# A decode attention kernel on one core: all K ahead of all V in shared buffers, MLP between the V groups, and four denominator matmuls for eight

## Chip, cores, metric

One NeuronCore of a Trainium2 chip. The metric is device time in microseconds of one execution. The profile's span (first to last instruction) is shorter than the time of the same execution in the kernel before (2.6 in its profile). Ratios compare runs of the same chip and call; where microseconds of two kernels are set against each other, the calls may differ, and the ratios to the kernel before say how far that holds. "Fast" means within 1.5% of the fastest of the same kernel, "slow" the rest.

## The reference, cut to what matters

```python
W = 1024                       # of 4096 cached positions, the last 1024
q = (layernorm(x) @ wq)        # B = 4, one new token, 32 query heads, 8 K/V heads, head size 128
scores = q @ k[:, :, -W:].T * 128 ** -0.5
o = softmax(scores) @ v[:, :, -W:]
s = o @ wo                     # 4096 -> 512
h = gelu(layernorm(xn) @ w1 + b1)        # 512 -> 1792
g = silu(h @ w2 + b2)                    # 1792 -> 512
return x + s * g
```

All is bf16. Per K/V head ("group") there is 1 MiB of K and 1 MiB of V over the four batch rows; wq and wo have 4 MiB each, w1 and w2 1.75 MiB each: 27.5 MiB (28.8 MB) to be read once, with little arithmetic.

## The kernel before: the parts concerned

Everything is requested from one queue, K and V alternating, four buffers each; a new K or V waits for the matmuls that free its buffer.

```python
NKN = 4; NV = 4; NKT = 6; NP = 3          # buffers: K, V, transposed K, probabilities
load_k(0)
d_wq = [...]                               # four DMAs of 1 MiB
load_v(0); load_k(1); d_w1 = ...; load_v(1); load_k(2); d_w2 = ...; load_v(2); load_k(3); load_v(3)
```

One unit is 256 positions of a group for all four batch rows: eight 128x128 transposes by the tensor engine (PE), one copy out of PSUM by the vector engine (DVE), eight score matmuls.

```python
def T(n): ...   # 8 transposes into psK, then a DVE copy to kt_buf
def S(n): ...   # 8 score matmuls (before the first of a group: a 512-column mask fill); after the 4th unit Exp on ACT
def PV(g):      # 32 matmuls v.T @ P, then the denominator:
    for k in range(8):
        pe.matmul(pso[:, 32:96], ones_bf, P_buf[:, g % NP, k * 64:(k + 1) * 64], ...)
for n in range(4, NUN + LAG + 1):          # LAG = 2
    T(n); S(n - LAG)
    if last unit of a group: PV(g - 1)     # mlp1 after the first, mlp3 after the second
    ...
rows1 = to_rows(0, 6)                      # head outputs, reshuffled for the projection
PV(7); ...
for k in range(3): wo(k, rows1)            # 96 projection matmuls, groups 0 to 5
rows2 = to_rows(6, 8)
for k in range(3, 6): wo(k, rows2)         # 32 more
```

The softmax here doesn't subtract the row's maximum and nothing guards it: scores larger than these inputs give would overflow.

Of the kernel before, what the change touches and what calls it, by code (L numbers as in the profile page):

```python
# [16 lines left out]
class _Program:  # L17
# [10 lines left out]
    def add(self, eng, fn, *deps):  # L28
        op = _Op(eng, fn, deps)
        self.ops[eng].append(op)  # L30
        return op
# [42 lines left out]
def bass_recurrent_scan__sliding_block_cached__mixer_channel_mlp__decode_kernel(  # L74
# [26 lines left out]
    FC = F // 128  # L101
# [1 line left out]
    KR = W // NC  # L103
    UT = 8
    NU = NC // UT
    NKN = 4
    NV = 4
    NKT = 6
    NP = 3
    NB = 3  # L110
    SCALE = DH ** -0.5
    GELU_A = 1.5957691216057308
# [39 lines left out]
    OW = sb([128, 4, HKV * 4], BF16)  # L152
    hT = sb([128, FC * 4], BF16)

    kn_buf = sb([128, NKN, NC, DH], BF16)
    v_buf = sb([128, NV, NC, DH], BF16)
    kt_buf = sb([128, NKT, UT * 128], BF16)
    P_buf = sb([128, NP, NC * 16], BF16)
    OTb = sb([128, HKV * 16], BF16)
    den_sb = sb([128, HKV * 16], F32)  # L160
    rden = sb([128, HKV * 16], F32)
# [31 lines left out]
    def cache_rows(cache, g):  # L193

        return bass.AP(cache.tensor, g * SK * DH + WS * DH,
                       [[NC * DH, KR], [HKV * SK * DH, B], [1, NC * DH]])
# [4 lines left out]

    def load_k(g):
        d_k[g] = pg.dma("sp", "k%d" % g, lambda e: e.dma_start(  # L203
            kn_buf[:, g % NKN, :, :].rearrange("p c d -> p (c d)"), cache_rows(A_k_cache, g)),
            t_last[g - NKN] if g >= NKN else None)

    def load_v(g):
        d_v[g] = pg.dma("sp", "v%d" % g, lambda e: e.dma_start(  # L208
            v_buf[:, g % NV, :, :].rearrange("p c d -> p (c d)"), cache_rows(A_v_cache, g)),
            pv_op[g - NV] if g >= NV else None)  # L210

    load_k(0)
    wq_r = A_wq.rearrange("(p c) n -> p c n", c=4)
    d_wq = [pg.dma("sp", "wq%d" % c, lambda e, c=c: e.dma_start(  # L214
        wq_sb[:, c, :], wq_r[:, c, :])) for c in range(4)]
    load_v(0)
    load_k(1)
    d_w1 = pg.dma("sp", "w1", lambda e: e.dma_start(
        w1_sb[:, :, :], B_w1.rearrange("(p c) f -> p c f", c=4)))
    load_v(1)  # L220
    load_k(2)
    d_w2 = pg.dma("sp", "w2", lambda e: e.dma_start(
        w2_sb[:, :, :], B_w2.rearrange("(p c) o -> p c o", c=FC)))
    load_v(2)
    load_k(3)
    load_v(3)

    x_r = A_x.rearrange("b s (c p) -> (b s c) p", p=128)


# [46 lines left out]
    def T(n):  # L277
        g, u = n // NU, n % NU

        def fn(pe):  # L280
            last = None
            for j in range(UT):
                last = pe.transpose(psK[n % NB][:, j * 128:(j + 1) * 128],  # L283
                                    kn_buf[:, g % NKN, u * UT + j, :], ident[:, :])
            return last
        t = add("pe", fn, d_k[g], c_id, cp.get(n - NB), v_xyT if n >= 4 else None)
        if u == NU - 1:
            t_last[g] = t
        cp[n] = add("dve", lambda e: e.tensor_copy(kt_buf[:, n % NKT, :], psK[n % NB][:, 0:1024]),  # L289
                    t, sc.get(n - NKT))  # L290

    def S(n):
        g, u = n // NU, n % NU

        def fn(pe):
            last = None
            if u == 0:
                pe.matmul(psS[g % 2][:, 0:512], ind[:, :], negm[:, :], start=True, stop=False,  # L298
                          skip_group_check=True)
            for j in range(UT):  # L300
                c = u * UT + j
                last = pe.matmul(psS[g % 2][:, c * 16:(c + 1) * 16],  # L302
                                 kt_buf[:, n % NKT, j * 128:(j + 1) * 128],
                                 qT[:, g * 16:(g + 1) * 16],
                                 start=False, stop=(c == NC - 1), skip_group_check=True)
            return last
        sc[n] = add("pe", fn, cp[n], v_q, c_neg, c_ind,
                    ex[g - 2] if u == 0 and g >= 2 else None)
        if u == NU - 1:
            ex[g] = add("act", lambda e: e.activation(  # L310
                P_buf[:, g % NP, :], psS[g % 2][:, 0:512], AF.Exp, scale=SCALE),
                sc[n], den[g - NP] if g >= NP else None)

    def PV(g):
        pso = psO[g % 2]

        def fn(pe):
            last = None
            for c in range(NC):
                last = pe.matmul(pso[:, 0:16], v_buf[:, g % NV, c, :],  # L320
                                 P_buf[:, g % NP, c * 16:(c + 1) * 16],
                                 start=(c == 0), stop=(c == NC - 1))
            return last
        pv_op[g] = add("pe", fn, ex[g], d_v[g], ep[g - 2] if g >= 2 else None)

        def fd(pe):
            last = None
            for k in range(8):
                last = pe.matmul(pso[:, 32:96], ones_bf[:, :],  # L329
                                 P_buf[:, g % NP, k * 64:(k + 1) * 64],  # L330
                                 start=(k == 0), stop=(k == 7))
            return last
        den[g] = add("pe", fd)

    def epilogue(g):
        pso = psO[g % 2]
        cs = slice(g * 16, (g + 1) * 16)
        v = add("dve", lambda e: e.tensor_reduce(  # L338
            den_sb[:, cs], bass.AP(pso, 32, [[512, 128], [1, 16], [16, 4]]),
            AX.X, ALU.add), den[g])  # L340
        v = add("dve", lambda e: e.reciprocal(rden[:, cs], den_sb[:, cs]), v)  # L341

        ep[g] = add("dve", lambda e: e.tensor_tensor(
            bass.AP(OTb, g * 16, [[HKV * 16, 128], [1, 4], [4, 4]]),
            pso[:, 0:16], rden[:, cs], ALU.mult), v, pv_op[g])


    v_xyT = None
    for n in range(4):
        T(n)  # L350

    def f_xy(pe):
# [3 lines left out]
                last = pe.transpose(psK[1][:, s + c * 4:s + c * 4 + 4],  # L356
                                    bass.AP(src, c, [[512, 4], [4, 128]]), ident[0:4, 0:4])
        return last
    t_xy = add("pe", f_xy, v_xn, v_y, c_id, cp[3])
    v_xyT = add("dve", lambda e: e.tensor_copy(xyT[:, :], psK[1][:, 0:32]), t_xy)  # L360

    def f_q(pe):
# [15 lines left out]
    def mlp1():  # L378
        def fn(pe):
            last = None  # L380
            for k in range(FC):
                o = psM[:, PS_H + k * 4:PS_H + (k + 1) * 4]
                for c in range(4):
                    pe.matmul(o, bass.AP(w1_sb, c * F + k, [[4 * F, 128], [FC, 128]]),  # L384
                              xyT[:, 16 + c * 4:16 + (c + 1) * 4], start=(c == 0), stop=False)
                last = pe.matmul(o, bass.AP(b1_sb, k, [[F, 1], [FC, 128]]), ones_bf[0:1, 0:4],  # L386
                                 start=False, stop=True)
            return last
        h = psM[:, PS_H:PS_H + FC * 4]
        t = add("pe", fn, v_xyT, d_w1, d_b1)  # L390
        a = add("act", lambda e: e.activation(u2_sb[:, :], h, AF.Square), t)  # L391
        v = add("dve", lambda e: e.tensor_scalar(t_sb[:, :], u2_sb[:, :], GELU_K, 1.0,  # L392
                                                 op0=ALU.mult, op1=ALU.add), a)
        v = add("dve", lambda e: e.tensor_tensor(t2_sb[:, :], t_sb[:, :], h, ALU.mult), v)
        mlp["e"] = add("act", lambda e: e.activation(ge_sb[:, :], t2_sb[:, :], AF.Exp,
                                                     scale=-GELU_A), v)

    def mlp2():
        h = psM[:, PS_H:PS_H + FC * 4]
        v = add("dve", lambda e: e.tensor_single_scalar(e1_sb[:, :], ge_sb[:, :], 1.0, ALU.add),  # L400
                mlp["e"])
        v = add("dve", lambda e: e.reciprocal(r_sb[:, :], e1_sb[:, :]), v)
        mlp["h"] = add("dve", lambda e: e.tensor_tensor(hT[:, :], h, r_sb[:, :], ALU.mult), v)
# [20 lines left out]
        mlp["g"] = add("dve", lambda e: e.tensor_tensor(  # L424
            g_sb[:, :], psM[:, PS_Z:PS_Z + 16], rz_sb[:, :], ALU.mult), v)

    LAG = 2
    NUN = HKV * NU
    for n in range(4, NUN + LAG + 1):
        g, u = n // NU, n % NU  # L430
        if n < NUN:
            T(n)
        if n - LAG < NUN:
            if n == 4:
                S(0)
                S(1)
            S(n - LAG)
        if u == NU - 1 and 1 <= g:
            PV(g - 1)
            if n == 7:  # L440
                mlp1()
            if n == 11:
                mlp3()
            if g - 1 + NV < HKV:
                load_k(g - 1 + NKN)
                load_v(g - 1 + NV)
        if u == 0 and g >= 2 and n < NUN:
            epilogue(g - 2)
        if n == 9:
            mlp2()  # L450
        if n == 14:
            mlp4()

    wo_r = A_wo.rearrange("(g p i) o -> p g i o", g=HKV, i=4)
    d_wo = []
# [41 lines left out]
            return last  # L497
        return add("pe", fn, d, rows, mlp["g"])

    rows1 = to_rows(0, 6)  # L500
    epilogue(HKV - 2)
    PV(HKV - 1)
    epilogue(HKV - 1)
    for k in range(3):
        wo(k, rows1)
    rows2 = to_rows(6, 8)
    for k in range(3, len(d_wo)):
        t_w = wo(k, rows2)


    v = add("dve", lambda e: e.tensor_tensor(
# [61 lines left out]
```

## Time and profile before

| | before |
|---|---|
| time, three runs | 80.37, 80.77, 80.80 us |
| span of the profiled execution (82.2 us, a slow one) | 79.6 us |
| bytes, mean rate from 2 to 70.5 us | 28.8 MB, 418 GB/s |
| last byte | about 72.0 us |
| end of the last projection matmul | 76.8 us |
| PE stops without a wait ("issue") of over half a us | 0.81, 1.96, 2.16 us |

In a line of the chain of waits, the first number is the start, the second the duration, then the engine, the tile written, and how many instructions were merged. "issue" is time for which the profile shows no reason. In a line by stage: window, its length, then busy time (and instructions) of PE, PE weight load, DVE, ACT, POOL, then clock, DMA share and GB/s. The lines themselves stand in the prediction below.

### The profile page before, as it was taken

The numbers are of one execution on the slowest core, as the hardware profiler recorded it, in microseconds if no ns is written. First come the engines' busy times: TensorE is split into PE (matmuls) and PEld (weight loads), VectorE is DVE, ScalarE is ACT, GpSimd is POOL, SyncE is SP. The second block draws the span as 40 slices with busy tenths as digits, with TensorE's granted clock in tenths as the row PEclk, the third lists the DMA queues.
The fourth block names the chain that finished last, engine by engine and source line by source line (L and its number), as shares of the span: only waits on it lengthen the run. The fifth ranks groups of instructions, "written<-read, shape, count | busy, mean of one in ns | idle before, by whom it ended". The sixth has DMA issues, their size and how long they took to land.

```text
span 79.6 us, 2723 instructions
## 1 busy us (share of the span) xinstructions
PE 56.5 (71%) x1267; PEld 52.9 (66%) x1267; DVE 32.7 (41%) x82; ACT 8.4 (11%) x15; POOL 4.3 (5%) x12
## 2 busy tenths in 40 slices
PE   0029510097089999999999999969819999708860
PEld 0029310096079999999899899969718999608850
DVE  0788900002033600029811886929636368403010
ACT  0617000000002000023000302003003020300000
POOL 6950000000000000000000000000000000000000
PEclk9999995555555999655697589999995599965555
DMA  0999999999999999999999999999999999971000
GB/s 2 339 425 401 433 424 428 424 424 460 412 425 416 420 429 446 402 416 412 437 420 437 399 437 416 420 404 420 424 408 420 410 414 422 414 286 56 0 0 2
DMA packets 4502, 29.01 MB, mean 365 GB/s; under 512 B 518, under 2 KB 523, under 8 KB 1676
## 3 DMA queue, kind: packets, MB, share of 16 engines
q1 hardware_dynamic: 4448, 28.84, 87.2%
q8 instruction: 9, 0.15, 0.7%
q10 hardware_dynamic: 44, 0.01, 0.1%
q14 instruction: 1, 0.01, 0.0%
HBM read 28.85 MB, written 0.00 MB: 363 GB/s over the span
## 4 chain that ended last, share of the span: by engine, by line
PE 62%; DMA 22%; issue 7%; SPq 4%; DVE 1%; ACT 1%
PE psK L283 23%; DMA kn_buf<-in_A_k_cache_dram 22%; PE psO L320 9%; PE psS L302 8%; PE psM L384 6%; PE psM L491 4%; PE psS L298 3%; PE psO L329 3%; SPq L214 3%; PE psM L386 3%; PE psM L411 2%; SPq L203 1%; ACT P_buf L310 1%; SPq L208 1%; PE psM L413 1%
## 5 line engine op out<-in xcount | busy, mean ns | idle before, releaser
L283 PE MATMUL psK<-ident,kn_buf 128*128 128x128 bf16 x256 | 25.3, 261 | 10.4 <-DMA kn_buf<-in_A_k_cache_dram 8.4
L289 DVE COPY kt_buf<-psK 128x1024 bf16<-128x1024 bf16 x32 | 21.2, 684 | 16.4 <-PE psK L283 16.4
L283 PEld LDWEIGHTS psK<-ident,kn_buf 128*128 128x128 bf16 x256 | 19.6, 118 | 10.8 <-DMA kn_buf<-in_A_k_cache_dram 8.5
L302 PEld LDWEIGHTS psS<-qT,kt_buf 128*128 128x128 bf16 x256 | 11.0, 103 | 1.8 <-issue 1.3
L302 PE MATMUL psS<-qT,kt_buf 128*128 128x16 bf16 x256 | 11.4, 174 | 0.0
L320 PE MATMUL psO<-P_buf,v_buf 128*128 128x16 bf16 x256 | 7.8, 170 | 2.6 <-issue 2.2
L310 ACT ACTIVATE P_buf<-psS 128x512 bf16<-128x512 f32 x8 | 4.8, 598 | 41.0 <-PE psS L302 41.0
L320 PEld LDWEIGHTS psO<-P_buf,v_buf 128*128 128x128 bf16 x256 | 7.1, 96 | 2.8 <-issue 2.2
L366 PE MATMUL psM<-xyT,wq_sb 128*128 128x4 bf16 x128 | 3.6, 166 | 5.4 <-DMA wq_sb<-in_A_wq_dram 5.4
L366 PEld LDWEIGHTS psM<-xyT,wq_sb 128*128 128x128 bf16 x128 | 3.5, 104 | 5.5 <-issue 5.5
L384 PE MATMUL psM<-xyT,w_sb 128*128 128x4 bf16 x56 | 5.6, 204 | 0.0
L384 PEld LDWEIGHTS psM<-xyT,w_sb 128*128 128x128 bf16 x56 | 4.4, 154 | 0.2
L298 PE MATMUL psS<-negm,ind 128*128 128x512 bf16 x8 | 4.0, 506 | 0.1
L329 PE MATMUL psO<-P_buf,ones_bf 128*128 128x64 bf16 x64 | 3.5, 197 | 0.8 <-issue 0.8
L372 DVE CAST qT<-psM 128x128 bf16<-128x128 f32 x1 | 0.4, 435 | 8.8 <-PE psM L366 8.8
L491 PE MATMUL psM<-OW,wo_sb 128*128 128x4 bf16 x128 | 3.7, 166 | 0.4 <-DVE OW L477 0.4
L491 PEld LDWEIGHTS psM<-OW,wo_sb 128*128 128x128 bf16 x128 | 3.6, 105 | 0.5 <-issue 0.5
L392 DVE TENSOR_SCALAR t_sb<-u_sb 128x56 f32<-128x56 f32 x1 | 0.2, 192 | 7.4 <-ACT u_sb L391 7.4
L329 PEld LDWEIGHTS psO<-P_buf,ones_bf 128*128 128x128 bf16 x64 | 2.6, 100 | 0.9 <-issue 0.9
L338 DVE TENSOR_REDUCE den_sb<-psO 128x16 f32<-128x64 f32 x8 | 1.7, 216 | 3.3 <-PE psO L329 3.3
L386 PE MATMUL psM<-ones_bf,b_sb 1*128 1x4 bf16 x14 | 3.0, 215 | 0.0
L341 DVE RECIPROCAL rden<-den_sb 128x16 f32<-128x16 f32 x8 | 2.0, 253 | 0.3
(57 smaller groups left out, 27.0 us busy)
## 6 DMA issues: line engine op xcount, KB each, us to landing
kn_buf<-in_A_k_cache_dram SPq DMA_DIRECT2D x8, 1024.0 KB, 19.7
v_buf<-in_A_v_cache_dram SPq DMA_DIRECT2D x8, 1024.0 KB, 17.1
wq_sb<-in_A_wq_dram SPq DMA_DIRECT2D x4, 1024.0 KB, 9.5
w_sb<-in_B_w_dram SPq DMA_DIRECT2D x2, 1792.0 KB, 24.7
wo_sb<-in_A_wo_dram SPq DMA_DIRECT2D x3, 1024.0 KB, 14.8
wo_sb<-in_A_wo_dram SPq DMA_DIRECT2D x1, 512.0 KB, 17.4
wo_sb<-in_A_wo_dram SPq DMA_DIRECT2D x2, 256.0 KB, 15.6
x<-in_A_x_dram ACTq DMA_DIRECT2D x2, 2.0 KB
```

What stands on the lines that cost most here:

```text
L214: d_wq = [pg.dma("sp", "wq%d" % c, lambda e, c=c: e.dma_start(wq_sb[:, c, :], wq_r[:, c, :])) for c in range(4)]
L283: last = pe.transpose(psK[n % NB][:, j * 128:(j + 1) * 128], kn_buf[:, g % NKN, u * UT + j, :], ident[:, :])
L289: cp[n] = add("dve", lambda e: e.tensor_copy(kt_buf[:, n % NKT, :], psK[n % NB][:, 0:1024]), t, sc.get(n - NKT))
L298: pe.matmul(psS[g % 2][:, 0:512], ind[:, :], negm[:, :], start=True, stop=False, skip_group_check=True)
L302: last = pe.matmul(psS[g % 2][:, c * 16:(c + 1) * 16], kt_buf[:, n % NKT, j * 128:(j + 1) * 128], qT[:, g * 16:(g + 1) * 16], start=False, ...
L310: ex[g] = add("act", lambda e: e.activation(P_buf[:, g % NP, :], psS[g % 2][:, 0:512], AF.Exp, scale=SCALE), sc[n], den[g - NP] if g >= NP ...
L320: last = pe.matmul(pso[:, 0:16], v_buf[:, g % NV, c, :], P_buf[:, g % NP, c * 16:(c + 1) * 16], start=(c == 0), stop=(c == NC - 1))
L329: last = pe.matmul(pso[:, 32:96], ones_bf[:, :], P_buf[:, g % NP, k * 64:(k + 1) * 64], start=(k == 0), stop=(k == 7))
L366: last = pe.matmul(psM[:, PS_Q + h * 4:PS_Q + (h + 1) * 4], wq_sb[:, c, h * DH:(h + 1) * DH], xyT[:, c * 4:(c + 1) * 4], start=(c == 0), s ...
L384: pe.matmul(o, bass.AP(w1_sb, c * F + k, [[4 * F, 128], [FC, 128]]), xyT[:, 16 + c * 4:16 + (c + 1) * 4], start=(c == 0), stop=False)
L386: last = pe.matmul(o, bass.AP(b1_sb, k, [[F, 1], [FC, 128]]), ones_bf[0:1, 0:4], start=False, stop=True)
L491: last = pe.matmul(psM[:, PS_W + c * 4:PS_W + (c + 1) * 4], wo_sb[:, g, i, c * 128:(c + 1) * 128], OW[:, i, g * 4:(g + 1) * 4], start=firs ...
```

## The change

The intent: get all scores done while K streams, keep the probabilities of all eight groups, and leave only short V work and the output projection for the end. K and V share eight buffers. The core of the diff:

```diff
-    NKN = 4
-    NV = 4
-    NKT = 6
-    NP = 3
+    NS = 8
+    LAG = 8
+    NKT = LAG + 2
@@ loads
     load_k(0)
+    load_k(1)
-    (wq in four DMAs, then V0, K1, w1, V1, K2, w2, V2, K3, V3)
+    (wq in two DMAs)
+    for g in range(2, HKV):
+        load_k(g)
@@ load_v: buffer (8 + g) % 8, freed by the transposes of K group g
-            pv_op[g - NV] if g >= NV else None)
+            t_last[(HKV + g) % NS] if HKV + g >= NS else None)
@@ denominator
-            for k in range(8):
-                last = pe.matmul(pso[:, 32:96], ones_bf[:, :],
-                                 P_buf[:, g % NP, k * 64:(k + 1) * 64],
+            for k in range(4):
+                last = pe.matmul(pso[:, 128:256], ones_bf[:, :],
+                                 P_buf[:, g, k * 128:(k + 1) * 128],
@@ main loop: T and S only; then V0, w1, V1, w2, V2 to V7, wo are requested
+    for n in range(LAG, NUN + LAG):
+        if n < NUN:
+            T(n)
+        S(n - LAG)
@@ end
+    for g in range(HKV):
+        PV(g)            # mlp1 after PV(0), mlp2 and mlp3 after PV(1), mlp4 after PV(2)
+        ...
+    rows = to_rows(0, HKV)
+    for k in range(len(d_wo)):
+        t_w = wo(k, rows)
```

More of the change, by code (lines that the diff above doesn't have):

```diff
@@ L153, in bass_recurrent_scan__sliding_block_cached__mixer_channel_mlp__decode_kernel @@
     hT = sb([128, FC * 4], BF16)
-    kn_buf = sb([128, NKN, NC, DH], BF16)
-    v_buf = sb([128, NV, NC, DH], BF16)
+    kv_buf = sb([128, NS, NC, DH], BF16)
     kt_buf = sb([128, NKT, UT * 128], BF16)
-    P_buf = sb([128, NP, NC * 16], BF16)
+    P_buf = sb([128, HKV, NC * 16], BF16)
     OTb = sb([128, HKV * 16], BF16)
@@ L203, in load_k @@
         d_k[g] = pg.dma("sp", "k%d" % g, lambda e: e.dma_start(
-            kn_buf[:, g % NKN, :, :].rearrange("p c d -> p (c d)"), cache_rows(A_k_cache, g)),
-            t_last[g - NKN] if g >= NKN else None)
+            kv_buf[:, g, :, :].rearrange("p c d -> p (c d)"), cache_rows(A_k_cache, g)),
+            )
     def load_v(g):
         d_v[g] = pg.dma("sp", "v%d" % g, lambda e: e.dma_start(
-            v_buf[:, g % NV, :, :].rearrange("p c d -> p (c d)"), cache_rows(A_v_cache, g)),
-            pv_op[g - NV] if g >= NV else None)
+            kv_buf[:, (HKV + g) % NS, :, :].rearrange("p c d -> p (c d)"), cache_rows(A_v_cache, g)),
+            t_last[(HKV + g) % NS] if HKV + g >= NS else None)
     load_k(0)
+    load_k(1)
     wq_r = A_wq.rearrange("(p c) n -> p c n", c=4)
     d_wq = [pg.dma("sp", "wq%d" % c, lambda e, c=c: e.dma_start(
-        wq_sb[:, c, :], wq_r[:, c, :])) for c in range(4)]
-    load_v(0)
-    load_k(1)
-    d_w1 = pg.dma("sp", "w1", lambda e: e.dma_start(
-        w1_sb[:, :, :], B_w1.rearrange("(p c) f -> p c f", c=4)))
-    load_v(1)
-    load_k(2)
-    d_w2 = pg.dma("sp", "w2", lambda e: e.dma_start(
-        w2_sb[:, :, :], B_w2.rearrange("(p c) o -> p c o", c=FC)))
-    load_v(2)
-    load_k(3)
-    load_v(3)
+        wq_sb[:, 2 * c:2 * c + 2, :], wq_r[:, 2 * c:2 * c + 2, :])) for c in range(2)]
+    for g in range(2, HKV):
+        load_k(g)
     x_r = A_x.rearrange("b s (c p) -> (b s c) p", p=128)
@@ L283, in fn @@
                 last = pe.transpose(psK[n % NB][:, j * 128:(j + 1) * 128],
-                                    kn_buf[:, g % NKN, u * UT + j, :], ident[:, :])
+                                    kv_buf[:, g, u * UT + j, :], ident[:, :])
             return last
-        t = add("pe", fn, d_k[g], c_id, cp.get(n - NB), v_xyT if n >= 4 else None)
+        t = add("pe", fn, d_k[g], c_id, cp.get(n - NB), v_xyT if n >= LAG else None)
         if u == NU - 1:
@@ L310, in S @@
             ex[g] = add("act", lambda e: e.activation(
-                P_buf[:, g % NP, :], psS[g % 2][:, 0:512], AF.Exp, scale=SCALE),
-                sc[n], den[g - NP] if g >= NP else None)
+                P_buf[:, g, :], psS[g % 2][:, 0:512], AF.Exp, scale=SCALE),
+                sc[n])
     def PV(g):
@@ L319, in fn @@
             for c in range(NC):
-                last = pe.matmul(pso[:, 0:16], v_buf[:, g % NV, c, :],
-                                 P_buf[:, g % NP, c * 16:(c + 1) * 16],
+                last = pe.matmul(pso[:, 0:16], kv_buf[:, (HKV + g) % NS, c, :],
+                                 P_buf[:, g, c * 16:(c + 1) * 16],
                                  start=(c == 0), stop=(c == NC - 1))
@@ L327, in fd @@
             last = None
-            for k in range(8):
-                last = pe.matmul(pso[:, 32:96], ones_bf[:, :],
-                                 P_buf[:, g % NP, k * 64:(k + 1) * 64],
-                                 start=(k == 0), stop=(k == 7))
+            for k in range(4):
+                last = pe.matmul(pso[:, 128:256], ones_bf[:, :],
+                                 P_buf[:, g, k * 128:(k + 1) * 128],
+                                 start=(k == 0), stop=(k == 3))
             return last
@@ L338, in epilogue @@
         v = add("dve", lambda e: e.tensor_reduce(
-            den_sb[:, cs], bass.AP(pso, 32, [[512, 128], [1, 16], [16, 4]]),
+            den_sb[:, cs], bass.AP(pso, 128, [[512, 128], [1, 16], [16, 8]]),
             AX.X, ALU.add), den[g])
@@ L348, in bass_recurrent_scan__sliding_block_cached__mixer_channel_mlp__decode_kernel @@
     v_xyT = None
-    for n in range(4):
+    for n in range(LAG):
         T(n)
@@ L358, in f_xy @@
         return last
-    t_xy = add("pe", f_xy, v_xn, v_y, c_id, cp[3])
+    t_xy = add("pe", f_xy, v_xn, v_y, c_id, cp[LAG - 1])
     v_xyT = add("dve", lambda e: e.tensor_copy(xyT[:, :], psK[1][:, 0:32]), t_xy)
@@ L425, in mlp4 @@
             g_sb[:, :], psM[:, PS_Z:PS_Z + 16], rz_sb[:, :], ALU.mult), v)
-    LAG = 2
     NUN = HKV * NU
-    for n in range(4, NUN + LAG + 1):
-        g, u = n // NU, n % NU
+    for n in range(LAG, NUN + LAG):
         if n < NUN:
             T(n)
-        if n - LAG < NUN:
-            if n == 4:
-                S(0)
-                S(1)
-            S(n - LAG)
-        if u == NU - 1 and 1 <= g:
-            PV(g - 1)
-            if n == 7:
-                mlp1()
-            if n == 11:
-                mlp3()
-            if g - 1 + NV < HKV:
-                load_k(g - 1 + NKN)
-                load_v(g - 1 + NV)
-        if u == 0 and g >= 2 and n < NUN:
-            epilogue(g - 2)
-        if n == 9:
-            mlp2()
-        if n == 14:
-            mlp4()
+        S(n - LAG)
+    load_v(0)
+    d_w1 = pg.dma("sp", "w1", lambda e: e.dma_start(
+        w1_sb[:, :, :], B_w1.rearrange("(p c) f -> p c f", c=4)))
+    load_v(1)
+    d_w2 = pg.dma("sp", "w2", lambda e: e.dma_start(
+        w2_sb[:, :, :], B_w2.rearrange("(p c) o -> p c o", c=FC)))
+    for g in range(2, HKV):
+        load_v(g)
     wo_r = A_wo.rearrange("(g p i) o -> p g i o", g=HKV, i=4)
@@ L498, in wo @@
         return add("pe", fn, d, rows, mlp["g"])
-    rows1 = to_rows(0, 6)
-    epilogue(HKV - 2)
-    PV(HKV - 1)
-    epilogue(HKV - 1)
-    for k in range(3):
-        wo(k, rows1)
-    rows2 = to_rows(6, 8)
-    for k in range(3, len(d_wo)):
-        t_w = wo(k, rows2)
+    for g in range(HKV):
+        PV(g)
+        if g == 0:
+            mlp1()
+        if g >= 1:
+            epilogue(g - 1)
+        if g == 1:
+            mlp2()
+            mlp3()
+        if g == 2:
+            mlp4()
+    epilogue(HKV - 1)
+    rows = to_rows(0, HKV)
+    for k in range(len(d_wo)):
+        t_w = wo(k, rows)
     v = add("dve", lambda e: e.tensor_tensor(
```

## The prediction

> **What bounds the kernel now.** I read the slices of the page first, to see which resource is never idle.
>
> ```profile
> PE   0029510097089999999999999969819999708860
> PEclk9999995555555999655697589999995599965555
> GB/s 2 339 425 401 433 424 428 424 424 460 412 425 416 420 429 446 402 416 412 437 420 437 399 437 416 420 404 420 424 408 420 410 414 422 414 286 56 0 0 2
> ```
>
> Each column is 2 us. The transfers run at one level from column 1 to column 34, although the tensor engine (PE) has holes at the left and is full only from column 11 on. Cutting the run into stages gives numbers for that.
>
> ```profile
> 5.50:22.00 16.50, 7.42 (x168) 7.00 (x168) 4.60 (x11) 1.49 (x2) 0.00 (x0) 0.70 1.02 426
> 22.00:51.00 29.00, 28.84 (x542) 27.20 (x543) 13.25 (x33) 3.04 (x7) 0.00 (x0) 0.76 1.00 421
> 71.00:72.00 1.00, 0.02 (x1) 0.02 (x1) 0.00 (x0) 0.00 (x0) 0.00 (x0) 0.50 0.53 199
> 72.00:73.00 1.00, 1.00 (x31) 1.00 (x31) 0.31 (x2) 0.00 (x0) 0.00 (x0) 0.50 0.05 18
> ```
>
> After the window come its length, the busy time of PE, of its weight loads, of the vector engine (DVE) and others, then clock, DMA share and GB/s. So: 9.1 us of PE idleness before 22 us, almost none until 51, the queue full throughout, and the last bytes at about 72.0. The span is 79.6, so 7.6 us follow the last byte. The chain of waits in order of time says what they are:
>
> ```profile
> 68.90 0.92 PE psO L320 x30
> 69.82 2.16 issue
> 71.98 0.20 PE psO L320 x2
> 72.18 0.44 PE psO L329 x8
> 72.62 2.54 PE psM L491 x96
> 75.16 0.26 PE psS L470 x15
> 75.44 0.20 DVE OW L477
> 75.78 1.02 PE psM L491 x32
> 76.82 0.20 DVE sg_sb L511
> ```
>
> PE stops inside the last value product, resumes at 71.98, and only then does all 128 output-projection matmuls, whose weights had nearly all landed. That projection could lie beneath the transfer and doesn't. The last part of the tail (76.80 to 79.6, 2.8 us) is scaling, transpose, sum and store.
>
> The stop is neither a tensor wait nor a buffer wait. I counted PE instructions (matmuls plus weight loads) up to each of the three stops:
>
> ```profile
> 0.00:52.00 52.00, 36.96 (x730) 34.79 (x731) 21.08 (x51) 6.01 (x11) 4.32 (x12) 0.77 0.97 404
> 0.00:58.50 58.50, 41.89 (x858) 39.41 (x858) 25.39 (x62) 6.61 (x12) 4.32 (x12) 0.80 0.97 405
> 0.00:71.50 71.50, 51.76 (x1112) 48.57 (x1113) 31.35 (x76) 8.40 (x15) 4.32 (x12) 0.80 0.97 404
> ```
>
> 1461, 1716 and 2225: apart by 255 and 509[...]. I read them as stops at the edges of instruction blocks (0.81, 1.96 and 2.16 us, 4.9 in all).
>
> Last, the groups, for the price of each operation:
>
> ```profile
> L283 PE MATMUL psK<-ident,kn_buf 128*128 128x128 bf16 x256 | 25.3, 261 | 10.4 <-DMA kn_buf<-in_A_k_cache_dram 8.4
> L289 DVE COPY kt_buf<-psK 128x1024 bf16<-128x1024 bf16 x32 | 21.2, 684 | 16.4 <-PE psK L283 16.4
> L329 PE MATMUL psO<-P_buf,ones_bf 128*128 128x64 bf16 x64 | 3.5, 197 | 0.8 <-issue 0.8
> ```
>
> A mean of overlapping matmuls is no cost, so I take costs from the chain: eight K transposes advance it 0.46 us at full clock and 0.87 at half clock; eight score matmuls 0.18 or 0.20; one score-bank fill 0.22 or 0.43; a value product (32 matmuls) 0.81 to 0.84.
>
> [...] 418 GB/s on average from 2 to 70.5 us[...]. In half-microsecond windows the clock changes here at about 25.7, 32.6, 39.4, 42.8, 46.2, 59.9 and 63.3: steps of one, two and four times 3.4[...].
>
> **The change part by part.**
> *Bytes.* None removed: 28.8 MB at 418 GB/s is 69 us, and the last byte stays at about 72.0. 1 MiB costs 2.51 us. Order now: K0, K1, wq (4 MiB), K2 to K7, V0, w1 (1.75), V1, w2 (1.75), V2 to V7, wo (4).
> *Start.* Before, wq was complete at 15.7; one more MiB ahead of it makes 18.3. Eight units of K instead of four are transposed in the hole before that, moving about 2 us of work off the later path. The q projection takes 3.55 us: 21.9, against 19.3 before. But K2 has then landed (20.8), where the old kernel waited until 22.16 for K1: no loss.
> *K loop.* 24 rounds of one transpose unit and one score unit. At half clock 0.87 + 0.20 = 1.07; at full clock PE needs 0.46 + 0.18 + a quarter of 0.22 = 0.70, with the DVE copy just beneath it (0.684). I choose 5 us cold at the start (before, rising took 3.6 to 4.7 us of dense work), 4.5 rounds, then 19.5 x 0.70 = 13.7: 40.6. The last eight score units with two fills: 1.9, so 42.5.
> *V phase.* V0 landed at 35.9, w1 at 40.3. First value product with denominator about 1.2: 43.7. MLP first layer, as in the trace (28.13 to 34.74), 6.6: 50.3. Second value product: 51.5. The activation chain (Square, two DVE, Exp, three DVE; 1.8 us of instructions, 2.2 with gaps) ends at 52.5, so PE waits about 1 us; second layer 2.1: 54.6. Five value products at 1.2: 60.6, about at V6's arrival (59.7). V7 lands at 62.2, its product ends at 63.4, sums and row shuffle about 1.6: 65.0. The projection then follows wo's arrival piece by piece.
> *Denominator.* 4 matmuls of 128 columns for 8 of 64: at full clock 4 x 56 = 0.22 for 0.25 us[...]. No gain[...]. The reduction reads 64 more elements[...]. Off the path.
> *P kept for every group.* Removes a wait that appears in no list of waits: 0.
> *End.* Last byte 72.0, eight projection matmuls 0.25, unchanged end piece 2.8: 75.1, with 75.2 from the arrivals above. Against 79.6 that is 4.5 us less: the 0.6 of last value product and denominator and the 3.8 of projection and shuffle that now lie under the transfer.
>
> **The rivals.**
> *PE becomes the bound.* Without waiting for V7, PE would be through with value products at 61.8; it must be by about 67.3 (72.4 less 3.6 of projection and 1.5 of shuffle) to meet the last byte, so it has 5.5 us in hand. Block stops as before (4.9) just fit. A K loop cold throughout adds 19.5 x 0.37 + 1.0 = 8.2 us and would end near 78; both together near 83.[...] For the stops: they fell where PE ran fast and full.
> *V stalls behind K in shared buffers.* V7 may be requested only after the last transposes (about 40.6, or 48 cold). Its bytes start at 59.7. Hidden by over 10 us; worth 0. If it did bind, the DMA rate would show a dip.
> *The tail was luck.* The last stop (2.16 us) may be smaller in the timed runs: the profiled execution took 82.2 us, the timed ones 80.4 to 80.8. Then the old tail is shorter and the gain about 3 us: 77.7.
>
> **Range and chances.** 80.77 less 4.5 is 76.3; some weight on the third rival makes 76.5. Low 75.0 (stream slightly faster, shorter store), high 79.0 (PE partly bound). Faster by over 2% means below 79.15: 0.86. Within 2%: 0.11, PE late by 3 to 6 us. Slower: 0.03.
>
> **What would show it.** Right: bytes flowing at about 418 GB/s until about 72 with no dip; PE holes from about 55 us on, ended by V and wo transfers; only some eight to sixteen projection matmuls after the last byte; span near 75. The first wrong step would show as: PE full from 22 us to the end (first rival; look at the clock row between 22 and 42 us); fewer GB/s between 40 and 62 (second); projection matmuls in one uninterrupted run of 128 at the end. The prediction is wrong if the K loop runs at 1.07 per round, or if block stops exceed 5.5 us.

The sum: a span of 79.6 - 4.5 = 75.1 us, a time of 80.77 - 4.5 = 76.3, put at 76.5. Terms of the denominator (its cost at half clock, a loss in waiting time, the cost of the longer reduction) were counted at nothing in the 4.5. The V phase's 1.2 us per group hold some 0.4 of denominator: four matmuls of 128 columns started 107 ns apart, as the transposes start at half clock in the trace of the kernel before. That the stream can hardly be made shorter, and that the clock would not stay low through the K loop, were my estimates and not shown.

## The result

Four runs: 77.47, 77.54 (fast), 79.00, 79.02 (slow); median 78.27 us, against 80.78 for the kernel before in its four. The ratio of the fast runs is 0.961 (95% interval 0.954 to 0.968). A ratio is the mean time of one kernel's fast runs over that of the other's of the same rounds, so not quite the ratio of the medians quoted. The profiled run is a fast one: 77.54 us, span 75.8.

The slices of its page, 1.9 us each:

```profile
PE   0009995003996989999999499999689979838850
PEclk9999999855555559999999995555555555555555
GB/s 2 279 398 411 447 458 424 432 458 385 419 415 419 428 445 411 419 419 430 437 420 433 419 428 389 437 424 419 398 424 415 415 408 419 432 400 412 255 21 2
```

By stage:

```profile
5.50:22.00 16.50, 10.55 (x204) 10.33 (x205) 7.03 (x15) 1.49 (x2) 0.00 (x0) 0.78 1.01 429
22.00:51.00 29.00, 26.63 (x536) 25.53 (x541) 16.22 (x25) 4.78 (x8) 0.00 (x0) 0.79 1.01 421
72.00:73.00 1.00, 0.68 (x16) 0.55 (x16) 0.00 (x0) 0.00 (x0) 0.00 (x0) 0.50 0.13 43
```

The stream is what it was: 429 and 421 GB/s for 426 and 421, and it ends near 72; from 70.5 to 72.0 us it moves only 217 GB/s (209 before). PE works 3.1 us more before 22 us (10.55 for 7.42). The granted clock is 1.00 from 28.3 to 45.4 us and 0.50 afterwards. The end of the chain of waits (two pauses of 0.04 and 0.02 us left out):

```profile
54.55 18.07 DMA wo_sb<-in_A_wo_dram
72.67 0.39 PE psM L467 x8
73.08 0.20 DVE sg_sb L493
```

This is the picture the prediction drew: eight projection matmuls behind the last piece of wo instead of 128. That piece landed at 72.62, the matmuls ended at 73.06 (before: 76.80), and the unchanged scaling, transpose, sum and store follow. The groups:

```profile
L272 PE MATMUL psK<-ident,kv_buf 128*128 128x128 bf16 x256 | 23.1, 251 | 6.4 <-DMA kv_buf<-in_A_k_cache_dram 5.7
L278 DVE COPY kt_buf<-psK 128x1024 bf16<-128x1024 bf16 x32 | 21.1, 689 | 4.6 <-PE psK L272 4.5
L318 PE MATMUL psO<-P_buf,ones_bf 128*128 128x128 bf16 x32 | 4.7, 302 | 0.0
```

The denominator matmuls are half as many; their busy sum is larger (4.7 for 3.5 us), but matmuls overlap (mean 302 ns each, started 107 ns apart) and these ran at half clock, so this is no cost. And the block stops are not gone. Cutting the counts of PE instructions (matmuls plus weight loads) at three stops of the changed kernel:

```profile
0.00:43.30 43.30, 29.57 (x596) 28.66 (x603) 26.00 (x46) 6.55 (x10) 4.32 (x12) 0.84 0.96 400
0.00:62.40 62.40, 47.27 (x977) 45.38 (x985) 31.27 (x69) 8.40 (x15) 4.32 (x12) 0.75 0.97 405
0.00:68.70 68.70, 51.79 (x1104) 49.46 (x1111) 33.82 (x79) 8.40 (x15) 4.32 (x12) 0.73 0.98 406
```

1199, 1962 and 2215: apart by 763 and 253. In the timeline of the kernel before, exactly 128 matmuls stand between the end of its first stop and its second (52.51 to 57.44 us), with their weight loads 256 instructions. I take that for one block, and the 763 for three less a few lost records (the page has 1212 matmuls for 1219 weight loads). The stops there are 1.03, 0.53 and 0.26 us. The last edge lies 107 matmuls before the end of the projection, so no further block is needed.

### The profile page after: what moved, and what is told of

Read it like the earlier page. It is cut to its first block, busy times and chain, and to the rows that moved or that the text cites. A ratio compares the mean times of both kernels' runs of the same rounds, so it can differ in the third digit from the quotient of the medians.

```text
span 75.8 us, 2618 instructions
## 1 busy us (share of the span) xinstructions
PE 55.8 (74%) x1212; PEld 52.8 (70%) x1219; DVE 34.3 (45%) x81; ACT 8.4 (11%) x15; POOL 4.3 (6%) x12
## 4 chain that ended last, share of the span: by engine, by line
DMA 44%; PE 31%; SPq 19%; issue 3%; DVE 1%
DMA wo_sb<-in_A_wo_dram 24%; DMA wq_sb<-in_A_wq_dram 20%; PE psK L272 18%; SPq L435 16%; PE psS L291 7%; PE psM L355 5%; SPq L201 2%; SPq L213 1%; PE psS L497 1%; PE psM L467 1%; SPq L206 0%; DVE o_bf L499 0%; DVE sg_sb L493 0%
## 5 line engine op out<-in xcount | busy, mean ns | idle before, releaser
L272 PE MATMUL psK<-ident,kv_buf 128*128 128x128 bf16 x256 | 23.1, 251 | 6.4 <-DMA kv_buf<-in_A_k_cache_dram 5.7
L272 PEld LDWEIGHTS psK<-ident,kv_buf 128*128 128x128 bf16 x256 | 18.7, 114 | 6.5 <-DMA kv_buf<-in_A_k_cache_dram 5.7
L291 PE MATMUL psS<-qT,kt_buf 128*128 128x16 bf16 x256 | 10.6, 171 | 1.7 <-issue 1.4
L291 PEld LDWEIGHTS psS<-qT,kt_buf 128*128 128x128 bf16 x256 | 9.9, 99 | 2.4 <-issue 1.7
L309 PE MATMUL psO<-P_buf,kv_buf 128*128 128x16 bf16 x256 | 8.4, 175 | 0.5 <-issue 0.5
L309 PEld LDWEIGHTS psO<-P_buf,kv_buf 128*128 128x128 bf16 x256 | 8.1, 105 | 0.6 <-issue 0.6
L318 PE MATMUL psO<-P_buf,ones_bf 128*128 128x128 bf16 x32 | 4.7, 302 | 0.0
L327 DVE TENSOR_REDUCE den_sb<-psO 128x16 f32<-128x128 f32 x8 | 2.3, 289 | 3.5 <-PE psO L318 3.5
L400 PE MATMUL psM<-hT,w_sb 128*128 128x4 bf16 x56 | 2.1, 167 | 1.0 <-DVE hT L392 1.0
L400 PEld LDWEIGHTS psM<-hT,w_sb 128*128 128x128 bf16 x56 | 1.8, 105 | 1.3 <-DVE hT L392 1.2
```

What stands on the lines that cost most here:

```text
L272: last = pe.transpose(psK[n % NB][:, j * 128:(j + 1) * 128], kv_buf[:, g, u * UT + j, :], ident[:, :])
L291: last = pe.matmul(psS[g % 2][:, c * 16:(c + 1) * 16], kt_buf[:, n % NKT, j * 128:(j + 1) * 128], qT[:, g * 16:(g + 1) * 16], start=False, ...
L309: last = pe.matmul(pso[:, 0:16], kv_buf[:, (HKV + g) % NS, c, :], P_buf[:, g, c * 16:(c + 1) * 16], start=(c == 0), stop=(c == NC - 1))
L318: last = pe.matmul(pso[:, 128:256], ones_bf[:, :], P_buf[:, g, k * 128:(k + 1) * 128], start=(k == 0), stop=(k == 3))
L400: pe.matmul(o, w2_sb[:, k, c * 128:(c + 1) * 128], hT[:, k * 4:(k + 1) * 4], start=(k == 0), stop=False)
```

## The experiments

Theories at the start. **Tail**: the time is the end of the stream (about 72.6) plus what must follow the last byte (3.2 us of span), so long as PE is done. **PE-bound rival**: PE's work sets the end and the gain comes from filling its idle time and from fewer instructions. A third, **supply**, was formed on the way: while the stream runs, PE gets its instructions in blocks of 256 at no more than one per some 6 us, and their number counts rather than their work. Kernels of the name "old" vary the kernel before, "new" the changed one. All results were correct.

### 1. The end content put back: wo requested ahead of V7

```diff
-    for g in range(2, HKV):
+    for g in range(2, HKV - 1):
         load_v(g)
     (the six wo DMAs)
+    load_v(HKV - 1)
```

> Changed kernel with one thing moved: all of the output projection's weights are requested ahead of the last V group, so that the last byte belongs to V7. Tail theory: behind the last byte now lie a value product with denominator (about 1.3), sums and shuffle (1.8), 128 projection matmuls (3.6 to 3.9) in place of eight matmuls (0.4): 6.3 to 6.6 us more, about 84. Rival, the gain comes from filling tensor idleness earlier and from fewer instructions: no change, 77.5 to 79.

Measured: 83.83 us (83.79 to 83.96), ratio to before 1.035; 6.3 us over the changed kernel's fast runs. The chain:

```profile
63.99 8.53 issue
72.53 1.00 PE psO L309 x32
73.53 0.45 PE psO L318 x4
75.67 3.57 PE psM L468 x128
```

Same work, same instructions, one request moved: the value product and all 128 projection matmuls now follow the last byte. (The chain calls the 8.5 us before V7 "issue"; I take it that PE is waiting for V7 there, the only thing that was moved.) The tail theory got this right to 0.2 us, and PE-bound (no change) is out for this end of the kernel.

### 2. The changed kernel again, and the denominators taken off PE

The first repeats the kernel unchanged. In the second, DVE sums the 32 chunks of each group and one matmul makes all denominators:

```diff
-            for k in range(4):
-                last = pe.matmul(pso[:, 128:256], ones_bf[:, :], P_buf[:, g, k * 128:(k + 1) * 128], ...)
+    ps = [chunk_sum(g) for g in range(HKV)]     # DVE tensor_reduce over 32 chunks, rounded once to bf16
+    pe.matmul(psS[1][:, 0:128], ones_bf, psum_bf, start=True, stop=True)     # once, after mlp1
```

> The changed kernel once more, to see how its runs divide. So far it had two runs at 77.5 us and two at 79.0. Tail theory (the time is the end of the stream plus 3.2 us, as long as the tensor engine is done by then): most runs at 77.5, and any run at 79.0 is one in which the tensor engine came late. If the 79.0 runs instead come from a slower stream, they are unrelated to the tensor engine's work and would appear as often in every variant of this batch.

> Changed kernel with the denominators taken off the tensor engine: the vector engine sums each group's 32 chunks (it idles after 42 us), and one matmul of 128 columns for all groups takes the place of 32. That takes about 31 x 0.107 = 3.3 us of half-clock tensor work out of the V phase. Tail theory: the stream sets the end, so the fast runs stay at 77.5 (within 0.5 us), while runs at 79.0 become rare. Rival, tensor engine is the bound throughout: time falls by about 3 us to 74.5.

Measured: "again" 77.46, 77.56, 77.69 and 78.70 to 78.96 (four of seven, the profiled one among them). Without the denominators 77.53 to 77.64 (four runs), 78.92, and one profiled execution of 180.21 us, told below. I ran that kernel once more for a usable profile:

> The variant whose denominators the vector engine sums, unchanged, once more, since the profiled execution of the first time was an outlier of 180 us and left no usable profile. The stream sets the end: 77.5; the profile should show waits for V and for wo in the V phase, more than the 0.5 us of the changed kernel, and the last wo piece landing at 72.6 in a fast run or 74.0 in a slow one.

Measured: 77.48 to 77.59 (four) and 78.82 to 79.25 (four, the profiled one among them). The fast level is 77.5 with or without 31 matmuls: the stream is the bound there, as the tail theory says. The slow level is not clearly rarer: 5 of 13 executions (the outlier left out), against 6 of 11 of the changed kernel. So "a run at 79.0 is one in which PE came late" fell. In the slow profile of the kernel without PE denominators:

```profile
71.40 0.97 PE L455 MATMUL psM<-OW,wo_sb 128*128 128x4 bf16 x24 [0.23 <-DMA wo_sb<-in_A_wo_dram]
74.02 0.37 PE L455 MATMUL psM<-OW,wo_sb 128*128 128x4 bf16 x8 [1.66 <-DMA wo_sb<-in_A_wo_dram]
```

PE stands still 1.66 us for the last piece of wo, which lands at 73.97; in the slow profile of the unchanged kernel it lands at 74.04, in the fast one at 72.62. The 1.4 us between the levels is a late last piece. The kept traces say more, in their list of DMA packets, which no view prints. In the two slow profiles an instruction packet of 16 KB ran from 71.58 to 72.55 and from 71.83 to 72.79 us, and the last packets of wo follow directly on it, until 73.63 and 73.56. In two fast ones (the changed kernel and experiment 8) the same packet began only at 72.23 and 72.12, and the last data had moved by 72.25 and 72.21. So a slow run looks like one in which the instruction packet got ahead of the last data; this is read from four traces, and no experiment moved it.

The outlier: throughout its span of 178.5 us it had matmuls at a third of the half-clock pace (eight transposes advance the chain 2.72 us, against 0.87), though the record says a clock of 1.0. It happened once in the 61 executions of variants, and I have no explanation. It shows one thing of use, on its row of GB/s:

```profile
GB/s 191 429 434 411 428 424 430 430 419 439 90 0 235 0 0 239 0 0 233 2 0 193 46 0 136 99 2 88 395 418 282 0 0 4 0 4 0 4 0 1
```

With PE that slow, V seems to stall behind K's buffers: the line that requests K and V waited for PE eight times, 112.8 us in all, and the row shows one burst per group. That is the prediction's second rival, real in kind and absent at PE's normal pace.

### 3. Denominators computed twice

```diff
+            for r in range(2):
                 for k in range(4):
                     last = pe.matmul(pso[:, 128:256], ...)
```

> Changed kernel with each group's denominator computed twice (the second overwrites the first, result unchanged): 32 more matmuls of 128 columns, 32 x 0.107 = 3.4 us more tensor work in the V phase. The prediction put 5.5 us of room between the tensor engine and the last byte: then the time stays at 77.5. The profile after shows only about 1.3 us of waiting in the V phase and projection apart from the MLP chain: then about 2.1 us more, 79.6. If the tensor engine is the bound already: 3.4 more, 80.9.

Measured: 79.59 us (79.46 to 79.82), as expected of a room of about 1.3 us. But the reading was wrong, as experiments 5 and 6 show: there is a stop of 0.84 us in the shuffle and one of 0.69 us eleven matmuls before the end, at the places where block edges fall in a kernel with 64 more instructions.

### 4. Only the order of the old tail, only the new denominator on the old kernel

```diff
     rows1 = to_rows(0, 6)
     epilogue(HKV - 2)
+    for k in range(3):
+        wo(k, rows1)
     PV(HKV - 1)
     epilogue(HKV - 1)
-    for k in range(3):
-        wo(k, rows1)
```

> The kernel before with one thing moved: the 96 projection matmuls of groups 0 to 5 stand ahead of the last value product in the tensor engine's order, all else (interleaved K and V, early MLP) as before. Tail theory: what counts is only how much work stands behind the last byte (72.0), not K first; 2.5 us of projection leave the tail, and the instruction-block stop falls elsewhere: 80.7 - 2.5 = 78.2, most of the change's gain. Rival, K-first streaming or shared buffers matter by themselves: no more than 1 us of gain, 79.7 or above.

Measured: 81.11 us (80.76 to 81.65), ratio 1.004 (0.999 to 1.009): nothing. A miss. Its chain:

```profile
69.50 1.83 issue
71.33 1.90 PE psM L491 x66
73.23 0.86 PE psO L320 x32
```

PE stops at 69.50 as before and gets its next block at 71.33. Behind that edge stand 66 + 32 + 8 + 16 + 32 = 154 matmuls; behind the old kernel's edge (71.98) stand 2 + 8 + 96 + 16 + 32 = 154 too. Reordering instructions behind a block that has not come does not help.

The second kernel has the change's four denominator matmuls and the reduction for them, and nothing else:

> The kernel before with the change's denominator alone (4 matmuls of 128 columns for 8 of 64). Prediction: 0.22 for 0.25 us per group at full clock[...]: no gain, 80.7 within 1%. Rival, fewer matmuls help: 0.5 to 1 us less.

Measured: 79.28 us (79.12 to 79.47), ratio 0.981 (0.975 to 0.986): 1.6 us less from a part that the prediction valued at nothing. The array does the same columns (4 x 128 = 8 x 64), and its time hardly fell: from the first denominator matmul to the next matmul after the group it is 0.22 us for 0.23 at full clock, and 0.38 for 0.40 at half. What fell is the number of instructions, by 64. The stops in its chain, the lines between left out:

```profile
57.42 1.01 issue
58.43 0.29 PE psK L283 x2
63.67 1.14 issue
64.81 0.17 PE psS L302
69.13 1.73 issue
70.86 2.13 PE psM L491 x74
```

PE resumes at 58.43, 64.81 and 70.86: one block per 6.38 and 6.05 us. Each time it had finished the 256 instructions 1.0 to 1.7 us too early. Behind the last stop stand 74 + 16 + 32 = 122 matmuls instead of 154. (With their weight loads 154 matmuls are 308 instructions, more than one block, so the old kernel has one more edge after it; its profile shows no stop there.) One thing else differs: in this profile the transposes of K1 begin at 20.79 us, in those of the other old kernels at 22.16 to 22.35. How much of the 1.6 us that early arrival made isn't separated here; experiment 7, with 22.24, gains without it.

### 5. The old denominator on the changed kernel

```diff
-            for k in range(4):
-                last = pe.matmul(pso[:, 128:256], ...)
+            for k in range(8):
+                last = pe.matmul(pso[:, 32:96], ...)
```

> The changed kernel with the denominator as before (8 of 64 columns).[...] Tail theory: the stream sets the end, fast runs stay at 77.5. Tensor engine as the bound: 76.1.

Measured: 79.58 us (79.47 to 79.77), ratio 0.985 (0.980 to 0.989): 2.1 us slower than the changed kernel's fast runs, though its array work is nearly the same: 8 matmuls of 64 columns start 53 ns apart at half clock and 4 of 128 start 107 ns apart, 0.40 us for 0.38 until the next matmul. The cost of the old denominator at half clock, the ground of the 76.1 here (77.5 less 1.4): no trace shows it, and these 0.40 us contradict it. Both theories of the start missed. The chain shows 117 projection matmuls, a stop of 1.51 us from 72.92 on, and then the last 11: PE resumed at 62.80, 68.89 and 74.42, again about 6 us apart, and the last 22 instructions had to wait for a block of their own.

So with the two parts separated: order without denominator 1.3 us (80.87 to 79.58), denominator without order 1.6 us (80.87 to 79.28), both 3.1 to 3.4 us (fast means 80.65 to 77.51 and, in experiment 2, 80.97 to 77.57). In spans the same steps are smaller: 0.7 (78.26 to 77.60), 0.9 (78.26 to 77.38) and, from experiment 2, 2.7 us (78.47 to 75.80). The rest lies between span and time, where no view reaches.

### 6. Instructions added where PE only waits

This tells supply from work. Tiny matmuls stand where PE waits for wq anyway (in the profiles at 12.99 to 13.94 us, and at 10.60 to 13.22 in the old kernel); no busy stage gets more work.

```diff
+    def f_pad(pe):
+        for _ in range(32):            # 96 in the old kernel
+            last = pe.matmul(psO[0][:, 0:4], ident[:, :], ident[:, 0:4], start=True, stop=True)
     t_q = add("pe", f_q, v_xyT, *d_wq)
```

> The changed kernel with 32 matmuls of 4 columns (64 instructions) added where the tensor engine only waits for wq (14 to 18 us), so that no work is added to any busy stage. Block theory: the tensor engine gets its instructions in blocks of 256, about one per 6 us while the stream runs; the added 64 move the last block edge from 107 to 11 matmuls before the end, as in the variant with eight denominator matmuls, and a stop of about 1.5 us appears there: 79.5. Any theory in which only the work of the busy stages counts (tail, or tensor engine as bound): 77.5, unchanged.

Measured: 79.46, 79.61, 79.79 and one run at 81.43; ratio 0.986 (0.980 to 0.992). The expected 79.5 was met, 2 us above the changed kernel, and the stop is where it was expected:

```profile
69.53 3.26 PE psM L473 x117
72.79 1.78 issue
74.57 0.47 PE psM L473 x11
```

Sixty-four instructions in an idle stretch, almost 60 us earlier, cost 2 us at the end. No theory of work gives that. The last edge moved from 107 to 11 matmuls before the end, by 192 instructions for the 64 added: together 256 again. In this profile wq also came 1.3 us later (the q projection starts at 19.53 for 18.22), but that is not the cause: the value products began at 44.73, against 44.92 in the changed kernel. A second stop, of 1.69 us at 46.41, belongs to the moved edges as well, and PE begins the projection at 69.53 for 67.81. The 2 us show too (79.62 against 77.59 in experiment 8, fast means).

> The kernel before with 96 matmuls of 4 columns (192 instructions, that is 64 less than a block) added in the same wait for wq. Block theory: the block edges stand where the four-matmul denominator put them (22 matmuls into the projection), so the late stop falls early enough and the time is that of the old kernel with the new denominator, 79.3, although work was added and none taken out. If that variant's gain came from the denominator's own time: 80.8.

Measured: 80.37, 80.42, 80.59, one run at 81.68; ratio 0.996 (0.990 to 1.002). A miss: the block edges moved to where they were wanted (122 matmuls behind the last one, as in the kernel of 79.3), yet the time is nearly that of the old kernel. PE resumes at 59.95, 66.11 and 72.14, one block per 6.16 and 6.03 us, but the whole series is 1.3 to 1.5 us later than in experiment 4. By as much (1.4 us) the transposes of K1 began later, at 22.17 for 20.79, which I had overlooked. So the place of the edge alone is not it: how many blocks PE still has to be given from about 52 us on counts, and when that series starts.

### 7. Fewer instructions still, same array work

```diff
+            for k in range(2):
+                last = pe.matmul(pso[:, 128:384], ones_bf[:, :], P_buf[:, g % NP, k * 256:(k + 1) * 256], ...)
```

on the old kernel, with the reduction to match. That the array work is the same, the profile shows: from the first denominator matmul to the next matmul after the group it is 0.21 us at full clock and 0.38 at half, for 0.22 and 0.38 with four.

> The kernel before with the denominator in 2 matmuls of 256 columns per group: 96 instructions fewer than the kernel before and 32 fewer than with four matmuls, but the same array time (2 x 256 = 4 x 128 = 8 x 64 columns); the reduction on the vector engine reads 256 elements, somewhat longer. Supply theory (from about 52 us on the old kernel's tensor engine lives on one block of 256 instructions per 6.1 us): 96 / 256 x 6.1 = 2.3 us less than before, 78.5 (four matmuls: 1.5 less, 79.3 measured). If the gain of the four-matmul denominator came only from where its block edges fell: no further gain or a loss, 79.3 to 80.8. If array time decides: 80.8.

Measured: 78.21 to 79.41, median 78.84 us, ratio 0.972 (0.965 to 0.979). Eight, four and two matmuls give ratios of 1, 0.981 and 0.972 on the old kernel: the direction holds. The second step (some 0.7 us) agrees with 32 / 256 x 6.1 = 0.8; the whole comes to about 2.3 (0.028 x 80.8), as expected. The runs scatter more than in experiment 4, so the second step is not sharp.

### 8. Less transposed ahead of the q projection

```diff
-    LAG = 8
+    LAG = 4
```

> The changed kernel with four units of K transposed ahead of the q projection in place of eight, so that four units (about 2 us at full clock) return to the time after 22 us. Prediction (5.5 us of room): 77.5. With about 1 us of room, as the profile after shows: 78.5 to 79. Block edges don't move in the tail.

Measured: 77.42, 77.64, 77.72, one slow run of 79.19: unchanged. PE then runs the last 107 projection matmuls in one go to 72.95, without a wait for wo, and with a block stop of 0.26 us ahead of them:

```profile
69.51 0.26 issue
69.77 3.18 PE psM L467 x107
72.97 0.20 DVE sg_sb L493
```

So PE arrives just with the stream, and about 2 us of array work moved into the busy part cost nothing. (The profile's mean clock is 0.82 for 0.71, but a run at 0.72 took 77.72 us as well.) The room in work is larger than experiment 3 seemed to say; what there was none of is room in instructions.

A variant with ten shared K/V buffers, to see whether V ever waits for a K buffer, does not fit the on-chip memory and was not run (the build stopped at the transposed K, which needs 20480 bytes where 19552 were left).

## Why the prediction was right or wrong

The time fell into the range (78.27 for 75.0 to 79.0; the fast runs 77.5 for a centre of 76.5), and the picture of the tail was right. In one respect the number was luck: with a denominator worth nothing, as predicted, the kernel is that of experiment 5, at 79.58, outside the range. Point by point:

- **Stream** (last byte at 72.0, unchanged): right within 0.6 us. The last piece landed at 72.62, with no dip in the rate.
- **Tail** (eight projection matmuls plus 2.8 us after the last byte, span 75.1): right in kind, 75.8 measured. Experiment 1 shows that the content behind the last byte sets the end.
- **Start** (q projection ends at 21.9): right, 21.77.
- **K loop and V phase** (42.5, then waits for V6 and V7): 2.4 us off. The value products began at 44.9 and never waited for a V, so the PE holes ended by V transfers that were to show the prediction right did not come. Block stops of 0.64 and 1.03 us in the K loop, which I had put aside as rival, are in that. The clock rose at 28.3 us, 6.5 us after the loop began, where I had chosen 5. How the clock answers to transposes was not shown: in the kernel before it stayed full after the 3.4 us from 49.62 to 53.04 with 1.1 us of transposes, but fell after those from 56.45 to 59.86 with 1.3 us.
- **The 4.5 us** was too large. Fast against fast it was 3.1 to 3.4 us. The third rival holds: the profile of the kernel before is of a slow run, and the fast runs of later calls have spans of 77.9 to 79.4, mostly near 78.3, not 79.6. So the span that the prediction started from was about 1.3 us too long, and the last piece came 0.6 us later than predicted; against that stand the 0.7 us or so that the change won between span and time (2.2 to 2.9 us before, 1.7 to 1.9 after), which nothing here explains. No fast run of the old kernel was profiled.
- **Denominator, "No gain"**: this step failed. Its own chain shows 0.44 us for the eight of 64 columns (72.18 to 72.62), and the array time is nearly equal at either clock (0.22 for 0.23 and 0.38 for 0.40 us), so there was nothing to lose. And its 64 instructions were worth 1.6 us on the old kernel (79.28) and 2.1 us on the changed one (79.58 against 77.5).
- **"it has 5.5 us in hand"** and **"Block stops as before (4.9) just fit"**: the unit was wrong. I set stops, a given sum, against room in time. What the runs show is a supply of about one block per 6 us (where stop followed stop while the stream ran, PE resumed every 6.0 to 6.9 us; after 4.7 and 5.5 us in experiments 3 and 5, where the second came after the stream's end): 64 more instructions, placed where PE idles (experiment 6), use up the room and 2 us more, and 2 us of array work (experiment 8) do not.
- **P kept for every group, shared buffers**: 0 was predicted. Neither was run alone. No wait for them appears, and the outlier shows only that V would stall if PE were three times slower.

What the change does, then: it puts the projection under the stream, and the fewer instructions let PE's last block come early enough to use that. Each alone gives less than half or about half of the whole. No experiment beat the changed kernel's fast level of 77.5; below it lie only the stream and the 3.2 us after it.

That a stop is PE waiting for instructions rests on four things: edges 256 apart (253, 255, 509 and 763 recorded instructions), no tensor it waits for, the effect of instructions without work, and the instruction transfers (9 packets, 0.15 MB, 16 KB each on the page). Which packet ended which stop no view shows, but the packet lists in the kept traces do: all 41 stops of over 0.25 us that the chains of 13 traces call "issue", the wait for V7 in experiment 1 left out, ended 1.2 to 1.6 us after an instruction packet had landed. (The outlier's trace is not among them.) They also divide the 6 us: while the stream runs, the next packet starts 3.4 to 4.4 us after PE resumes and takes about 1.0 us, and PE resumes 1.2 to 1.6 us after it lands. Where PE resumed at 70.9 us or later, as the stream ran out, the next packet started after only 1.1 to 1.5 us. So most of the 6 us looks like waiting behind the stream. No experiment varied the stream's rate to prove it.

## What to carry to other kernels

In a kernel whose transfers never pause, first ask what stands behind the last byte, and move all of it but the last piece's share ahead. Then count PE instructions, not only their time: here, with tiny matmuls under a stream of 420 GB/s, merging eight into four of double width was worth as much (1.6 us alone) as reordering the whole kernel (1.3 us alone). Look too at where the last block edge falls: with 11 matmuls behind it the stop there was 0.69 to 1.78 us in three kernels here, with 107 behind it 0.26. A part that costs nothing by its busy time can still be tested alone cheaply.
